# Key sums as three additions and a reordered opening, in an attention and spectral-gate kernel on Trainium2

## The chip, the core and the metric

The kernel runs on one core of one Trainium2 chip. A core has TensorE (PE in the profile; its weight loads are PEld), VectorE (DVE), ScalarE (ACT), GpSimd (POOL) and the queue engine SyncE (SP), which here issues most DMA transfers. The metric is the device time of one execution in microseconds (us); a run's time is compared by the median over runs.

## The reference, cut to what matters

```
q, k, v: (4, 8, 768, 64)                    # batch, heads, tokens, head size
k_rep = k.reshape(4, 8, 12, 64, 64).mean(axis=3)        # one mean key per block of 64 tokens
gate = einsum("bhsd,bhnd->bhsn", q, k_rep)               # causal over blocks
mask: each token sees its 3 best blocks by gate and its own block, causally
attn = softmax(q @ k^T / 8 where mask) @ v
x = attn as (4, 768, 512)
x1, x2, x3 = split(x @ w_proj)
y = x1 * irfft(rfft(x2) * rfft(filter)) * x3
out = y @ w_out
```

The mean keys need, for each head, the sum of the tokens of every block. How that sum is begun is one half of the change.

## The kernel before, in words

The four batches have eight heads each. Two heads make a *pair*; there are 16 pairs (0 to 15), and every pair is worked in six *slots* (two heads times three groups of score tiles), 96 slots in all. In a slot, `scores` makes score tiles on TensorE, `exponentials` (L441) takes them through ScalarE's exponential (L445) and GpSimd's causal cut (L448), and `products` (L454) multiplies them with the values on TensorE (L466). After the third group of a head, VectorE divides by the row sums into `xnat` (L474, L475), which frees the accumulator. When all four pairs of a batch are done, the steps of `hyena` for that batch are put between the slots of the next one: matrix products, transforms with cosine and sine matrices, and products on VectorE and GpSimd (L541 to L558, L574, L594).

The preparation of a pair runs some slots ahead of it, by three lists written out by hand (`early`, `bank`, `fills`) that the slot loop empties: `prep_k16` (L304), `prep_k` (L316), `prep_kr` (L339), `prep_q` (L347), `prep_gate` (L374), `prep_mask` (L387), `prep_turn` (L400) and `prep_v` (L335). The order of the instructions on every engine is the program's order.

Keys arrive in `k_nat` as 96 partitions by 2 heads by 8 tokens by 64 numbers (each partition has eight neighbouring tokens). `prep_k16` does two things with them: a cast to 16 bits in `k16` (L309 on GpSimd, for pair 0 L311 on ScalarE), and the sum over the eight tokens in `ks` (L313, one `tensor_reduce` on VectorE over a view in which the token is innermost, with a stride of 64 numbers). `prep_k` multiplies `ks` with block indicators on TensorE (L319, `krp`), turns `k16` by transposes (L326, `kt`), copies them with ScalarE to `KH` (L329), and puts two transfers into a list `late` that copy `KH` to the score operands KA (first head) and KB (second head). `flush` issues what the list holds, on SP's queue. The score operands have 64 rows of keys or queries and 12 more: on the keys' side block indicators (`erow`, L199 to L204), on the queries' side the mask. The queries' operands are TQ (first head) and QB (second head); for pairs 0 and 1 QB's rows are copied from PSUM directly (L361 to L370), for the others by a transfer (L372).

The opening is written out in L90 to L222 and L635 to L666. It loads the first keys, queries, second keys and first values, makes small tables on GpSimd (`blk`, `half1`, `biasr`, `ownm`, `erow`), and the sine matrix FS in three parts: `sine_products` on TensorE and a rounding step on VectorE (L137), `sine_multiple` on GpSimd (L144), and `sine_rest`, a product on TensorE (L149) and the sine on ScalarE (L150). `warm(n)` is n products of zeros on TensorE (L100). `constants_late` is ten small VectorE instructions (L209 to L220). `second_buffers` (L663) sends `erow` to KA[1], KB[1] and KB[2] in slot 0 on SP's queue.

The tile `hsb` of the filter's spectrum (L274) has the tag `h0` or `h1` in a pool of two buffers, in slots 16 to 25.

Of the kernel before, what the change touches and what calls it, by code (L numbers as in the profile page):

```python
# [18 lines left out]
def kernel(  # L19
# [10 lines left out]
    nc = tc.nc  # L30

    B, H, S, D = q.shape
    P = 128
    SC = S // P
    NB = S // 64
# [39 lines left out]
    def load(p, what):  # L75
        b, dc = divmod(p, DC)
        src = {"k": k, "q": q, "v": v}[what]
        if what == "k":

            t = nat.tile([SE, 2, 8, D], FP32, name="k_nat", tag="k_nat", bufs=2)  # L80
            for h in range(2):
                nc.sync.dma_start(t[:, h], src[b, 2 * dc + h].rearrange("(p e) d -> p e d", e=8))
            nats[what, p] = t
            return
        t = nat.tile([P, SC, 2, D], FP32, name=what + "_nat", tag=what + "_nat")
        for h in range(2):
            nc.sync.dma_start(t[:, :, h, :], src[b, 2 * dc + h].rearrange("(c p) d -> p c d", p=P))
        nats[what, p] = t

    for p, w in ((0, "k"), (0, "q"), (1, "k"), (0, "v")):  # L90
        load(p, w)


# [36 lines left out]
    def sine_products(i):  # L130
        if i != 1:
            sine["t"] = sc_tile()
        pr = sine["t"][:, 512 * (i % 2):512 * (i % 2) + F]
        nc.tensor.matmul(pr, lhsT=tvals[:, P * i:P * (i + 1)], rhs=fvals, start=True, stop=False,
                         skip_group_check=True)
        ka = hy.tile([P, F], FP32, name="dft_ka", tag=f"t{i % 2 + 1}", bufs=3)
        nc.vector.tensor_scalar(ka, in0=pr, scalar1=1.0 / S2, scalar2=MAGIC,  # L137
                                op0=ALU.mult, op1=ALU.add)
        sine[i] = pr, ka

    def sine_multiple(i):
        pr, ka = sine[i]
        kw = hy.tile([P, F], fp, name=f"dft_kw{i}", tag="gg", bufs=2 * DC)
        nc.gpsimd.tensor_scalar(kw, in0=ka, scalar1=-MAGIC, scalar2=1.0, op0=ALU.add, op1=ALU.mult)  # L144
        sine[i] = pr, kw

    def sine_rest(i):
        pr, kw = sine.pop(i)
        nc.tensor.matmul(pr, lhsT=idn, rhs=kw, start=False, stop=True, skip_group_check=True)  # L149
        nc.scalar.activation(FS[:, i, :], pr, AF.Sin, bias=0.0, scale=TWO_PI / S2)  # L150

    nc.scalar.activation(tw, twf, AF.Sin, bias=0.0, scale=math.pi / S)
    for i in range(HC):
        sine_products(i)
    warm(5)

    idn = const.tile([P, P], fp, name="idn")
    nc.gpsimd.tensor_scalar(idn, in0=id32, scalar1=-float(S2), scalar2=0.0, op0=ALU.mult, op1=ALU.add)
    par = const.tile([P, 1], FP32, name="par")
    nc.gpsimd.iota(par, pattern=[[1, 1]], base=0, channel_multiplier=1,  # L160
                   allow_small_or_imprecise_dtypes=True)
    for i in range(HC):
        sine_multiple(i)
    blk = const.tile([SE, NB], FP32, name="blk")
    nc.gpsimd.memset(blk, 1.0)
    nc.gpsimd.affine_select(out=blk, in_=blk, compare_op=ALU.is_ge, fill=0.0, base=0,
# [13 lines left out]
    nc.gpsimd.memset(half1[0:1, :], 1.0)  # L180
    nc.gpsimd.memset(half1[32:33, 64:128], 1.0)
    biasr = const.tile([P, SC - 1, 2, NB], BF16, name="biasr")
    nc.gpsimd.memset(biasr, 0.0)
    for c in range(1, SC):
        nc.gpsimd.memset(biasr[0:1, c - 1, :, 2 * c + 1:NB], -CBIG)
        nc.gpsimd.memset(biasr[32:33, c - 1, :, 2 * c + 1:2 * c + 2], CBIG)

    MN = [const.tile([P, SC, P], fp, name=f"MN{i}") for i in range(2)]
    V16 = [const.tile([P, SC, 2, 66], fp, name=f"V16_{i}") for i in range(3)]
# [2 lines left out]
    TQ = [const.tile([P, S], fp, name=f"TQ{i}") for i in range(2)]  # L192
    QB = [const.tile([P, S], fp, name=f"QB{i}") for i in range(2)]
    ownm = const.tile([P, SC - 1, 2, NB], fp, name="ownm")
    nc.gpsimd.memset(ownm, 1.0)
    for c in range(1, SC):
        for hf in range(2):
            nc.gpsimd.memset(ownm[64 * hf:64 * hf + 64, c - 1, :, 2 * c + hf:2 * c + hf + 1], 0.0)
    erow = KA[0][64:64 + NB, :]  # L199
    nc.gpsimd.memset(erow, MKEY)  # L200
    nc.gpsimd.affine_select(out=erow, in_=erow, compare_op=ALU.is_ge, fill=0.0, base=0,
                            pattern=[[1, S]], channel_multiplier=-64)
    nc.gpsimd.affine_select(out=erow, in_=erow, compare_op=ALU.is_ge, fill=0.0, base=63,
                            pattern=[[-1, S]], channel_multiplier=64)  # L204

    def constants_late():
        parh = const.tile([P, 1], FP32, name="parh")
# [11 lines left out]
        nc.vector.memset(tw0[0:1, 0:1], 0.0)  # L219
        nc.vector.memset(tw0[0:1, 1:2], 1.0 / S)  # L220

    nc.vector.memset(MN[0], 0.0)  # L222
    sgn = const.tile([P, 1], FP32, name="sgn")
    tw0 = const.tile([P, 2], FP32, name="tw0")
    flip = const.tile([P, P], FP32, name="flip")
# [68 lines left out]
    state = {}  # L294
# [9 lines left out]
    def prep_k16(p):  # L304
        kn = nats["k", p]
        k16 = hp.tile([SE, 8, 2, D], fp, name="k16", tag="k16")
        src = kn.rearrange("p h e d -> p e h d")
        if p:
            nc.gpsimd.tensor_copy(k16, src)  # L309
        else:  # L310
            nc.scalar.copy(k16, src)  # L311
        ks = small.tile([SE, 2, D], FP32, name="ks", tag="ks")
        nc.vector.tensor_reduce(out=ks, in_=kn.rearrange("p h e d -> p h d e"), axis=AX.X, op=ALU.add)  # L313
        state["k", p] = k16, ks

    def prep_k(p):  # L316
# [30 lines left out]
    def prep_q(p, t):  # L347
        qn = nats["q", p]
        tq = TQ[p % 2]
        if t == 0:  # L350
            state["ql", p] = hp.tile([P, S], fp, name="ql", tag="ql")
        ql = state["ql", p]
        qt = turned_pair("qt", qn, t)
        cols = slice(F * t, F * (t + 1))
        nc.scalar.activation(tq[:, cols], qt, AF.Copy, bias=0.0, scale=QS)  # L355
        lo = P if t == 0 else 0
        nc.vector.scalar_tensor_tensor(out=ql[:, F * t + lo:F * (t + 1)], in0=qt[:, lo:F],  # L357
                                       scalar=QS, in1=tq[:, F * t + lo:F * (t + 1)],
                                       op0=ALU.mult, op1=ALU.subtract)
        if p < 2:  # L360
            def direct():  # L361
                if p:
                    nc.vector.tensor_scalar(QB[p][0:D, cols], in0=qt[D:P, :], scalar1=QS,
                                            scalar2=None, op0=ALU.mult)
                else:
                    nc.scalar.activation(QB[p][0:D, cols], qt[D:P, :], AF.Copy, bias=0.0, scale=QS)
            if p:
                direct()
            else:
                state["direct", t] = direct  # L370
        elif t == 1:
            late.append(lambda: nc.sync.dma_start(QB[p % 2][0:D, :], tq[D:P, :]))  # L372

    def prep_gate(p):  # L374
# [25 lines left out]
    def prep_turn(p):  # L400
        mn, tq, qb = MN[p % 2], TQ[p % 2], QB[p % 2]
        mt = one("mt", (P, SC, P), fp)
        for c in range(SC):
            nc.tensor.transpose(mt[:, c, :], mn[:, c, :], id16)  # L404
        if p < 2:
            flat = mt.rearrange("p c s -> p (c s)")
            nc.scalar.activation(tq[64:64 + NB, :], flat[64:64 + NB], AF.Copy, bias=0.0, scale=MQ)
            nc.vector.tensor_scalar(qb[64:64 + NB, :], in0=flat[96:96 + NB], scalar1=MQ,
                                    scalar2=None, op0=ALU.mult)
        else:  # L410
            m16 = hp.tile([P, S], fp, name="m16", tag="m16")
            nc.scalar.activation(m16[64:108, :], mt[64:108].rearrange("p c s -> p (c s)"),  # L412
                                 AF.Copy, bias=0.0, scale=MQ)
            late.append(lambda: (nc.sync.dma_start(tq[64:64 + NB, :], m16[64:64 + NB, :]),
                                 nc.sync.dma_start(qb[64:64 + NB, :], m16[96:96 + NB, :])))
# [216 lines left out]
        for f in todo:  # L632
            f()

    sine_rest(0)  # L635
    prep_k16(0)
    prep_k(0)
    flush()
    load(1, "q")
    prep_kr(0)  # L640
    prep_q(0, 0)
    prep_q(0, 1)
    sine_rest(1)
    sine_rest(2)
    nc.scalar.preload_act_table_set("natural_log_exp_and_others")
    prep_gate(0)
    prep_mask(0)
    state.pop(("direct", 0))()
    state.pop(("direct", 1))()
    for p, w in ((2, "k"), (1, "v"), (2, "q")):  # L650
        load(p, w)
    warm(8)
    prep_turn(0)
    warm(4)
    constants_late()
    nc.gpsimd.tensor_copy(KB[0][64:64 + NB, :], erow)
    for t in V16:
        nc.gpsimd.memset(t[:, :, :, D:D + 2], 1.0)
    prep_v(0)
    prep_k16(1)  # L660
    scores(0)

    def second_buffers():  # L663
        for t in (KA[1], KB[1], KB[2]):
            nc.sync.dma_start(t[64:64 + NB, :], erow)
        nc.vector.memset(MN[1], 0.0)  # L666


    early = [[] for _ in range(slots + 1)]
# [36 lines left out]
                at(bank, n0 + 8, lambda p=p: turn_x(p))  # L706
            at(early, n0 + 10, lambda p=p: fold(p))

    early[0].append(second_buffers)
    early[1].append(make_flip)  # L710
    early[3].append(cosines)
    for i in range(HC):
# [99 lines left out]
```

## Time and profile before

| | |
|---|---|
| runs, us | 297.91, 297.96, 302.45 (median 297.96) |
| profiled execution, us | 295.79 |
| its span, first to last instruction, us | 294.1 |
| busy: TensorE, VectorE, ScalarE, GpSimd, us | 247.2, 196.4, 171.0, 153.5 |
| share of the chain that ended last: TensorE, VectorE | 46%, 31% |
| first score product, first exponential, us from the start | 15.95, 16.53 |
| mean granted clock of TensorE | 0.95 |

The page of the profile gives the engines' busy times, the span in 40 slices, the chain of work that ended last (followed back from the last instruction, at each step to what released it) and the costliest groups of instructions. A group's row has the line, engine, operation, tile written and tiles read, partitions by elements, the count, the busy time in all and the mean of one in ns, and then the idle time of the engine in front of them and what ended it. A row of a timeline has start and duration in us, engine, line, operation and tiles. A row of the chain in order of time has start, duration, engine and line.

### The profile page before, as it was taken

The page shows a single profiled execution, that of the slowest core. Times are in us where ns is not written, and L with a number is a line of the kernel's source. Part 1 is how long each engine was busy: PE and PEld are TensorE (multiplying, and loading weights), DVE is VectorE, ACT ScalarE, POOL GpSimd, SP SyncE. Part 2 cuts the span into 40 slices and gives each one's busy share as a digit, 9 for nine tenths or more (in the row PEclk, how much of TensorE's full clock was granted, in tenths as well). Part 3 has the DMA queues.
Part 4 walks back from the last instruction along what each step waited for, and adds up shares of the span by engine and source line. Part 5 has one row for each costly group of instructions (what it writes and reads, how often), then busy time and mean ns, then how long its engine had stood idle before and what let it go on. Part 6 is the DMA issues. An engine that isn't in the chain of part 4 may idle for free.

```text
span 294.1 us, 6382 instructions
## 1 busy us (share of the span) xinstructions
PE 247.2 (84%) x2300; PEld 153.3 (52%) x2300; DVE 196.4 (67%) x531; ACT 171.0 (58%) x260; POOL 153.5 (52%) x285
## 2 busy tenths in 40 slices
PE   7869878868597969898979789889899998988874
PEld 1547655545464536555555466656455664534431
DVE  5477877769745996867186959593759764237580
ACT  2736594757284627586846467768665675442323
POOL 6835352659471757765324667672326876004740
PEclk9985798989599999999999999999999999999998
DMA  7585967666687755377845344477631102400005
GB/s 185 113 167 153 240 178 155 133 133 144 133 148 160 135 114 141 75 147 205 231 97 139 69 123 113 112 182 229 136 83 45 34 8 66 171 0 0 2 0 214
DMA packets 71991, 36.11 MB, mean 123 GB/s; under 512 B 59684, under 2 KB 65048, under 8 KB 71960
## 3 DMA queue, kind: packets, MB, share of 16 engines
q1 hardware_dynamic: 69704, 33.62, 46.1%
q0 software_dynamic: 2256, 2.10, 5.3%
q8 instruction: 18, 0.29, 0.4%
q14 instruction: 13, 0.11, 0.1%
HBM read 24.64 MB, written 6.29 MB: 105 GB/s over the span
## 4 chain that ended last, share of the span: by engine, by line
PE 46%; DVE 31%; ACT 11%; issue 6%; DMA 2%; POOL 2%; SPq 1%; POOLq 0%; DVEq 0%; ACTq 0%
DVE ks L313 6%; PE sps L436 6%; PE op L601 5%; PE o L466 4%; PE x1p L586 4%; PE x3p L589 4%; PE x2p L524 4%; ACT ex L445 4%; DVE m L392 3%; DVE xnat L475 3%; PE kt L326 2%; DVE ql L357 2%; PE qt L300 2%; PE xx L536 2%; DVE yy L574 2%
## 5 line engine op out<-in xcount | busy, mean ns | idle before, releaser
L445 ACT ACTIVATE ex<-sps 128x896 f16<-128x896 f32 x96 | 87.4, 925 | 3.9 <-PE sps L436 3.9
L448 POOL TENSOR_SCALAR_AFFINE_SELECT ex<-ex 128x256 f16<-128x256 f16 x96 | 39.8, 416 | 88.4 <-ACT ex L445 65.0
L466 PEld LDWEIGHTS <-ex 128*128 128x128 f16 x672 | 33.8, 101 | 36.0 <-DVE xnat L475 21.6
L466 PE MATMUL o<-V,ex 128*128 128x65 f16 x672 | 38.7, 199 | 13.7 <-DVE xnat L475 12.7
L436 PE MATMUL sps<-QB,KB 76*128 76x512 f16 (+1 forms) x144 | 28.2, 307 | 4.1 <-ACT ex L445 4.1
L313 DVE TENSOR_REDUCE ks<-k_nat 96x128 f32<-96x1024 f32 x16 | 30.7, 1922 | 0.0
L547 POOL TENSOR_TENSOR PQ<-ta 128x512 f16<-128x512 f32 x12 | 15.2, 1268 | 26.8 <-DVE ta L546 26.8
L412 ACT ACTIVATE m<-mt 44x768 f16<-44x768 f16 x14 | 11.3, 806 | 30.1 <-PE mt L404 30.0
L436 PE MATMUL sps<-TQ,KA 76*128 76x512 f16 (+1 forms) x144 | 27.2, 300 | 1.9 <-DMA TQ<-m 1.1
L601 PE MATMUL op<-wo,yT 128*128 128x512 f16 x96 | 24.2, 379 | 3.4 <-POOL yT L556 3.4
L524 PE MATMUL x2p<-wp,xf 128*128 128x512 f16 x96 | 24.3, 379 | 0.8 <-DVE xf L503 0.8
L357 DVE SCALAR_TENSOR_TENSOR ql<-qt,TQ 128x256 f16<-128x256 f32 (+1 forms) x32 | 15.5, 485 | 13.1 <-ACT TQ L355 12.9
L355 ACT ACTIVATE TQ<-qt 128x384 f16<-128x384 f32 x32 | 15.7, 492 | 13.7 <-PE qt L300 13.4
L594 DVE TENSOR_TENSOR gg<-x1sb,x3p 128x384 f32<-128x384 f16 x24 | 13.2, 549 | 14.6 <-ACT x1sb L592 7.6
L556 POOL TENSOR_TENSOR yT<-gg,yy 128x384 f16<-128x384 f32 x16 | 16.0, 998 | 11.5 <-DVE yy L574 11.4
L586 PE MATMUL x1p<-xT,wp 128*128 128x384 f16 x96 | 19.5, 325 | 2.6 <-DVE tb L542 2.6
L592 ACT CAST x1sb<-x1p 128x384 f16<-128x384 f32 x24 | 11.5, 480 | 17.0 <-PE x1p L586 16.7
L604 ACT COPY osb<-op 128x512 f32<-128x512 f32 x24 | 14.1, 588 | 11.3 <-PE op L601 9.5
L589 PE MATMUL x3p<-xT,wp 128*128 128x384 f16 x96 | 19.5, 326 | 1.1 <-ACT x1sb L592 1.1
L436 PEld LDWEIGHTS <-KB 76*128 76x128 f16 x144 | 13.4, 102 | 12.0 <-issue 6.5
L329 ACT COPY KH<-kt 128x768 f16<-128x768 f16 x16 | 12.8, 799 | 10.5 <-PE kt L326 10.0
L475 DVE TENSOR_TENSOR xnat<-o,rc 128x384 f16<-128x384 f32 x32 | 17.9, 558 | 1.1
(162 smaller groups left out, 529.6 us busy)
## 6 DMA issues: line engine op xcount, KB each, us to landing
k_nat<-in_k_dram SPq DMA_DIRECT2D x32, 192.0 KB, 3.3
q_nat<-in_q_dram SPq DMA_DIRECT2D x32, 192.0 KB, 4.0
v_nat<-in_v_dram SPq DMA_DIRECT2D x32, 192.0 KB, 4.7
out_dram<-osb SPq DMA_DIRECT2D x24, 256.0 KB, 2.2
KA<-KH SPq DMA_DIRECT2D x16, 96.0 KB, 2.1
KB<-KH SPq DMA_DIRECT2D x16, 96.0 KB, 2.2
wp<-in_moe_w_proj_dram POOLq DMA_DIRECT2D x12, 128.0 KB, 3.9
QB<-TQ SPq DMA_DIRECT2D x14, 96.0 KB, 2.1
```

What stands on the lines that cost most here:

```text
L313: nc.vector.tensor_reduce(out=ks, in_=kn.rearrange("p h e d -> p h d e"), axis=AX.X, op=ALU.add)
L357: nc.vector.scalar_tensor_tensor(out=ql[:, F * t + lo:F * (t + 1)], in0=qt[:, lo:F], scalar=QS, in1=tq[:, F * t + lo:F * (t + 1)], op0=ALU ...
L436: nc.tensor.matmul(t[:, col:col + q1 - q0], lhsT=kk[0:64 + NB, P * kc:P * (kc + 1)], rhs=qq[0:64 + NB, q0:q1], start=True, stop=True, skip ...
L445: nc.scalar.activation(ex, t[:, 0:W], AF.Exp, bias=0.0, scale=EXPS)
L448: nc.gpsimd.affine_select(out=tri, in_=tri, compare_op=ALU.is_ge, fill=0.0, base=0, pattern=[[0, 2], [1, P]], channel_multiplier=-1)
L466: nc.tensor.matmul(o[:, qc, :], lhsT=ex[:, c0:c0 + P], rhs=V16[p % 3][:, kc, h, 0:65], start=first, stop=False, skip_group_check=True)
L475: nc.vector.tensor_tensor(xn[:, :, D * h:D * (h + 1)], o[:, :, 0:D], rc.to_broadcast([P, SC, D]), op=ALU.mult)
L524: nc.tensor.matmul(pa, lhsT=xf[:, eo, dc, P * i:P * (i + 1)], rhs=wp[:, dc, Dm:2 * Dm], start=(dc == 0), stop=(dc == DC - 1))
L556: nc.gpsimd.tensor_mul(st["yT"][:, dc, 0:F], g, yy[:, 0, :])
L586: nc.tensor.matmul(x1p, lhsT=wp[:, d2, dsl], rhs=xT[:, d2, hs], start=(d2 == 0), stop=(d2 == DC - 1))
L589: nc.tensor.matmul(x3p, lhsT=wp[:, d2, 2 * Dm + P * dc:2 * Dm + P * (dc + 1)], rhs=xT[:, d2, hs], start=(d2 == 0), stop=(d2 == DC - 1))
L601: nc.tensor.matmul(op, lhsT=st["yT"][:, cc, P * i:P * (i + 1)], rhs=wo[:, cc, :], start=(cc == 0), stop=(cc == DC - 1))
```

## The change

It has two halves.

The sum over eight tokens becomes three additions of halves: tokens 0 to 3 and 4 to 7 into a tile `k4` (512 numbers a partition, from the pool and tag of `hsb`'s first buffer), its halves into `k2` (256), and those into `ks` (128). The cast of pair 0's keys goes from ScalarE to GpSimd, like that of the other pairs.

The opening is written in another order. Loads: first queries, first keys, second keys, first values, second queries. The rounding step of the sines goes from VectorE to ScalarE. The tables `biasr` and `ownm` go from GpSimd to VectorE, with the zeros of MN[0] behind them. The sines' multiples come behind the first keys' cast, and the queries' transposes ahead of the keys' product. The three `sine_rest` come behind the first gates and masks. `erow`, its copy to KB[0] and `par` come behind these (`mask_rows`). QB's rows of pairs 0 and 1 go by a transfer like the others'. The mask rows of TQ for pair 0 are copied by VectorE. There are fewer warm-up products (3, 4 and 2 in place of 5, 8 and 4). The three transfers of `erow` to the other operands are issued in slots 1, 4 and 7.

```diff
-    for p, w in ((0, "k"), (0, "q"), (1, "k"), (0, "v")):
+    for p, w in ((0, "q"), (0, "k"), (1, "k"), (0, "v"), (1, "q")):
         load(p, w)
...
-        nc.vector.tensor_scalar(ka, in0=pr, scalar1=1.0 / S2, scalar2=MAGIC,
-                                op0=ALU.mult, op1=ALU.add)
+        nc.scalar.activation(ka, pr, AF.Copy, bias=MAGIC, scale=1.0 / S2)
...
-    warm(5)
+    warm(3)
...
-    for i in range(HC):
-        sine_multiple(i)
...
-    nc.gpsimd.memset(biasr, 0.0)
+    nc.vector.memset(biasr, 0.0)
     for c in range(1, SC):
-        nc.gpsimd.memset(biasr[0:1, c - 1, :, 2 * c + 1:NB], -CBIG)
-        nc.gpsimd.memset(biasr[32:33, c - 1, :, 2 * c + 1:2 * c + 2], CBIG)
+        nc.vector.memset(biasr[0:1, c - 1, :, 2 * c + 1:NB], -CBIG)
+        nc.vector.memset(biasr[32:33, c - 1, :, 2 * c + 1:2 * c + 2], CBIG)
...
-    nc.gpsimd.memset(ownm, 1.0)
+    nc.vector.memset(ownm, 1.0)
...
+    nc.vector.memset(MN[0], 0.0)
...
+    def mask_rows():
+        nc.gpsimd.memset(erow, MKEY)
+        nc.gpsimd.affine_select(out=erow, in_=erow, compare_op=ALU.is_ge, fill=0.0, base=0,
+                                pattern=[[1, S]], channel_multiplier=-64)
+        nc.gpsimd.affine_select(out=erow, in_=erow, compare_op=ALU.is_ge, fill=0.0, base=63,
+                                pattern=[[-1, S]], channel_multiplier=64)
+        nc.gpsimd.tensor_copy(KB[0][64:64 + NB, :], erow)
+        nc.gpsimd.iota(par, pattern=[[1, 1]], base=0, channel_multiplier=1,
+                       allow_small_or_imprecise_dtypes=True)
...
-        if p:
-            nc.gpsimd.tensor_copy(k16, src)
-        else:
-            nc.scalar.copy(k16, src)
+        nc.gpsimd.tensor_copy(k16, src)
         ks = small.tile([SE, 2, D], FP32, name="ks", tag="ks")
-        nc.vector.tensor_reduce(out=ks, in_=kn.rearrange("p h e d -> p h d e"), axis=AX.X, op=ALU.add)
+        k4 = hy2.tile([SE, 2, 4, D], FP32, name="k4", tag="h0")
+        k2 = small.tile([SE, 2, 2, D], FP32, name="k2", tag="k2", bufs=1)
+        nc.vector.tensor_add(k4, kn[:, :, 0:4], kn[:, :, 4:8])
+        nc.vector.tensor_add(k2, k4[:, :, 0:2], k4[:, :, 2:4])
+        nc.vector.tensor_add(ks, k2[:, :, 0], k2[:, :, 1])
...
-        if p < 2:
-            def direct():
-                if p:
-                    nc.vector.tensor_scalar(QB[p][0:D, cols], in0=qt[D:P, :], scalar1=QS,
-                                            scalar2=None, op0=ALU.mult)
-                else:
-                    nc.scalar.activation(QB[p][0:D, cols], qt[D:P, :], AF.Copy, bias=0.0, scale=QS)
-            if p:
-                direct()
-            else:
-                state["direct", t] = direct
-        elif t == 1:
+        if t == 1:
             late.append(lambda: nc.sync.dma_start(QB[p % 2][0:D, :], tq[D:P, :]))
...
-            nc.scalar.activation(tq[64:64 + NB, :], flat[64:64 + NB], AF.Copy, bias=0.0, scale=MQ)
+            if p:
+                nc.scalar.activation(tq[64:64 + NB, :], flat[64:64 + NB], AF.Copy, bias=0.0, scale=MQ)
+            else:
+                nc.vector.tensor_scalar(tq[64:64 + NB, :], in0=flat[64:64 + NB], scalar1=MQ,
+                                        scalar2=None, op0=ALU.mult)
...
-    sine_rest(0)
     prep_k16(0)
+    for i in range(HC):
+        sine_multiple(i)
+    prep_q(0, 0)
+    prep_q(0, 1)
     prep_k(0)
     flush()
-    load(1, "q")
     prep_kr(0)
-    prep_q(0, 0)
-    prep_q(0, 1)
-    sine_rest(1)
-    sine_rest(2)
-    nc.scalar.preload_act_table_set("natural_log_exp_and_others")
     prep_gate(0)
     prep_mask(0)
-    state.pop(("direct", 0))()
-    state.pop(("direct", 1))()
+    for i in range(HC):
+        sine_rest(i)
+    nc.scalar.preload_act_table_set("natural_log_exp_and_others")
+    mask_rows()
     for p, w in ((2, "k"), (1, "v"), (2, "q")):
         load(p, w)
-    warm(8)
+    warm(4)
     prep_turn(0)
-    warm(4)
+    warm(2)
     constants_late()
-    nc.gpsimd.tensor_copy(KB[0][64:64 + NB, :], erow)
...
-    early[0].append(second_buffers)
+    early[0].append(lambda: nc.vector.memset(MN[1], 0.0))
+    for i, t in enumerate((KA[1], KB[1], KB[2])):
+        early[3 * i + 1].append(lambda t=t: buffer_rows(t))
```

More of the change, by code (lines that the diff above doesn't have):

```diff
@@ L154 @@
         sine_products(i)
-    warm(5)
+    warm(3)
     idn = const.tile([P, P], fp, name="idn")
     nc.gpsimd.tensor_scalar(idn, in0=id32, scalar1=-float(S2), scalar2=0.0, op0=ALU.mult, op1=ALU.add)
-    par = const.tile([P, 1], FP32, name="par")
-    nc.gpsimd.iota(par, pattern=[[1, 1]], base=0, channel_multiplier=1,
-                   allow_small_or_imprecise_dtypes=True)
-    for i in range(HC):
-        sine_multiple(i)
     blk = const.tile([SE, NB], FP32, name="blk")
@@ L194 @@
     ownm = const.tile([P, SC - 1, 2, NB], fp, name="ownm")
-    nc.gpsimd.memset(ownm, 1.0)
+    nc.vector.memset(ownm, 1.0)
     for c in range(1, SC):
         for hf in range(2):
-            nc.gpsimd.memset(ownm[64 * hf:64 * hf + 64, c - 1, :, 2 * c + hf:2 * c + hf + 1], 0.0)
+            nc.vector.memset(ownm[64 * hf:64 * hf + 64, c - 1, :, 2 * c + hf:2 * c + hf + 1], 0.0)
+    nc.vector.memset(MN[0], 0.0)
     erow = KA[0][64:64 + NB, :]
[L200 to L204, printed above, removed]
+    par = const.tile([P, 1], FP32, name="par")
+    def mask_rows():
[7 more added lines that the diff above has]
+                       allow_small_or_imprecise_dtypes=True)
     def constants_late():
@@ L220, in constants_late @@
         nc.vector.memset(tw0[0:1, 1:2], 1.0 / S)
-    nc.vector.memset(MN[0], 0.0)
     sgn = const.tile([P, 1], FP32, name="sgn")
@@ L661, with buffer_rows @@
     scores(0)
[L663 to L666, printed above, removed]
+    def buffer_rows(t):
+        nc.sync.dma_start(t[64:64 + NB, :], erow)
     early = [[] for _ in range(slots + 1)]
```

## The prediction, made before the result

> **What bounds the kernel now.** I read the page's parts 1, 2, 4 and 5, then the chain in order of time, then the timelines of VectorE (DVE) and GpSimd (POOL) around the lines that the diff touches. First the page:
>
> ```profile
> span 294.1 us, 6382 instructions
> ...
> PE 247.2 (84%) x2300; PEld 153.3 (52%) x2300; DVE 196.4 (67%) x531; ACT 171.0 (58%) x260; POOL 153.5 (52%) x285
> ...
> PE 46%; DVE 31%; ACT 11%; issue 6%; DMA 2%; POOL 2%; SPq 1%; POOLq 0%; DVEq 0%; ACTq 0%
> DVE ks L313 6%; PE sps L436 6%; PE op L601 5%; PE o L466 4%; PE x1p L586 4%; PE x3p L589 4%; PE x2p L524 4%; ACT ex L445 4%; DVE m L392 3%; DVE xnat L475 3%; PE kt L326 2%; DVE ql L357 2%; PE qt L300 2%; PE xx L536 2%; DVE yy L574 2%
> ...
> L313 DVE TENSOR_REDUCE ks<-k_nat 96x128 f32<-96x1024 f32 x16 | 30.7, 1922 | 0.0
> ```
>
> TensorE is the busiest engine, but the chain that ended last is handed between it and VectorE. Its largest single line is L313, the reduction that the change replaces: 16 of 1.92 us. In the chain in order of time it stands whole nine times (pairs 1, 3, 5, 6, 7, 8, 11, 12, 15) and in part twice more (9 and 13). How it bounds, at pair 7:
>
> ```profile
> 86.22 1.95 DVE ks L313
> 88.17 0.79 DVE m L392 x10
> ...
> 90.27 0.57 DVE xnat L475
> ...
> 90.88 0.39 PE o L466 x7
> ```
>
> The reduction stands on VectorE ahead of the gate maxima and of `xnat`, and TensorE waits for `xnat` to free its accumulator. What the reduction gains or loses there, the span gains or loses.
>
> **The three additions, alone.** They process 512, 256 and 128 elements per partition instead of 1024. No row has exactly such an addition; the nearest are VectorE's two-tensor operations in float32:
>
> ```profile
> L594 DVE TENSOR_TENSOR gg<-x1sb,x3p 128x384 f32<-128x384 f16 x24 | 13.2, 549 | 14.6 <-ACT x1sb L592 7.6 <-PE x3p L589 7.0
> L541 DVE TENSOR_TENSOR ta<-xx,Asb 128x512 f32<-128x512 f32 x9 | 6.2, 686 | 1.1 <-PE xx L536 1.1
> ```
>
> From 384 to 512 elements is 137 ns, 1.07 ns an element, with about 140 ns fixed. So the additions take 0.69, 0.41 and 0.28 us; each needs the one before, and such a step costs 0.04 us (0.15 us operations follow each other by 0.19 in the rows of L209 below). Sum 1.46 us, a gain of about 0.45 us on each reduction. Eleven on the chain would give 5 us.
>
> The Trainium skill ("VectorE: DVE Perf Modes", Rules for kernel authors) calls `tensor_reduce` the slowest VectorE operation and advises restructuring it; by that alone the change is the 5 us gain, and rival A below is that case.
>
> **The three additions, beside GpSimd.** This decides. An addition reads two tensors in SBUF; the reduction read one. Look at what the trace has of VectorE operations with two SBUF inputs:
>
>
> ```profile
> 278.92 1.06 DVE L558 TENSOR_TENSOR yT<-gg,yy 128x384 f16<-128x384 f32 x1
> ...
> 285.54 0.56 DVE L558 TENSOR_TENSOR yT<-gg,yy 128x384 f16<-128x384 f32 x1
> ```
>
> ```profile
> 278.57 1.00 POOL L556 TENSOR_TENSOR yT<-gg,yy 128x384 f16<-128x384 f32 x1 [1.88 <-DVE yy L574]
> ```
>
> ```profile
> 66.66 0.93 DVE L289 SCALAR_TENSOR_TENSOR A<-hsb,tw,turn 128x512 f16<-128x512 f32 x1
> ```
>
> ```profile
> 66.64 0.41 POOL L448 TENSOR_SCALAR_AFFINE_SELECT ex<-ex 128x256 f16<-128x256 f16 x1 [0.46 <-DMA QB<-m]
> 66.99 1.28 POOL L337 CAST V<-v_nat 128x768 f16<-128x768 f32 x1
> ```
>
> The same L558 takes 0.56 us alone and 1.06 where GpSimd works: it ends at 279.98, 0.41 us after GpSimd's 279.57, and 0.4 us is the streaming of its 384 elements. L289 ends 0.54 us after GpSimd's 67.05, the streaming of 512. Then GpSimd's cast, begun at 66.99, takes 1.28 us and ends 0.68 after VectorE. So the two engines do not share: the one that comes second waits for the other's whole instruction, then streams. The reductions, beside the same GpSimd work, all take 1.77 to 1.96 us:
>
> ```profile
> L319 PE MATMUL krp<-blk,ks x32: 232/259/386, 7.6 to 214.6; 96*128 96x12 f32 x32
> L313 DVE TENSOR_REDUCE ks<-k_nat x16: 1769/1938/1956, 5.7 to 208.4; 96x128 f32<-96x1024 f32 x16
> ```
>
> (per line: shortest, median and longest in ns, first and last start in us).
>
> The Trainium skill ("SBUF — State Buffer", Who interferes with whom) states just this: a VectorE instruction with two SBUF inputs and a GpSimd instruction that reads SBUF take an exclusive lock, and a reduction never does. The trace agrees by the rows above.
>
> Now the changed line's own place. `prep_k16` puts GpSimd's cast of the same keys (L309) beside the sum, so the two meet by construction. Pairs 7, 8 and 9:
>
> ```profile
> 86.61 0.40 POOL L448 TENSOR_SCALAR_AFFINE_SELECT ex<-ex 128x256 f16<-128x256 f16 x1 [1.31 <-ACT ex L445]
> 86.96 1.03 POOL L309 CAST k<-k_nat 96x1024 f16<-96x1024 f32 x1
> ```
>
> ```profile
> 101.61 1.95 DVE L313 TENSOR_REDUCE ks<-k_nat 96x128 f32<-96x1024 f32 x1
> ```
>
> ```profile
> 101.14 1.27 POOL L549 TENSOR_TENSOR PQ<-tb 128x512 f16<-128x512 f32 x1
> ```
>
> ```profile
> 118.11 1.96 DVE L313 TENSOR_REDUCE ks<-k_nat 96x128 f32<-96x1024 f32 x1
> ```
>
> ```profile
> 117.34 1.00 POOL L556 TENSOR_TENSOR yT<-gg,yy 128x384 f16<-128x384 f32 x1
> 118.30 1.01 POOL L558 TENSOR_TENSOR yT<-gg,yy 128x384 f16<-128x384 f32 x1
> ```
>
> I let the earlier comer go first. After a wait GpSimd has about 0.13 us of its instruction behind it (the cast above: 0.68 left of the usual 0.82), so L448 takes 0.27 more, L309 0.90 and L558 0.87; VectorE's additions take 0.54, 0.28 and 0.14 after a wait. Times from the start of the sum:
> - Pair 7: first addition to 0.69, L448 to 0.96, second to 1.24; the third is issued at 1.28, but L309 has been waiting and goes to 2.14; third to 2.28. Against 1.94: 0.34 lost. Pairs 5, 6, 11 and 15 have the same neighbours: 5 x 0.34 = 1.7 us.
> - Pair 8: L549 holds until 0.81; first to 1.35, L448 1.62, second 1.90, L309 2.80, third 2.94: 1.0 lost. Pair 12 is alike: 2.0 us.
> - Pair 9: L556 until 0.23; first 0.77, L558 1.64, second 1.92, L448 2.19, third 2.33: 0.39 lost; pair 13 alike: 0.8 us.
> - Pair 3 has two casts of 0.2 us ahead of L309 that let the third addition through: a gain of 0.35.
>
> Sum over the pairs behind the opening: +4.1 us. GpSimd ends its cast some 0.4 us later, hidden: the keys are transposed two slots later. Bounds: no meeting at all gives -0.45 x 10 = -4.5; GpSimd first at every meeting gives +8.4 (rival B). I take +4.1, by the rows' own order.
>
> **The opening.** These rows carry it:
>
> ```profile
> 0.81 0.87 SPq L82 DMA_DIRECT2D k_nat<-in_k_dram  x2
> ...
> 1.73 1.02 SPq L87 DMA_DIRECT2D q_nat<-in_q_dram  x2
> ...
> 13.67 0.82 DVE L398 TENSOR_TENSOR MN<-lt,ownm 128x120 f16<-128x120 f16 x1
> ...
> 15.93 0.56 DVE L408 TENSOR_SCALAR QB<-mt 12x768 f16<-12x768 f16 x1 [1.44 <-ACT TQ L407]
> 15.95 0.92 PE L436 MATMUL sps<-TQ,KA 76*128 76x512 f16 x6
> ...
> 16.50 0.15 DVE L209 TENSOR_SCALAR parh<-par 128x1 f32<-128x1 f32 x1
> ...
> 16.69 0.15 DVE L210 TENSOR_SCALAR parh<-parh 128x1 f32<-128x1 f32 x1
> ...
> 17.78 1.87 DVE L313 TENSOR_REDUCE ks<-k_nat 96x128 f32<-96x1024 f32 x1
> ...
> 19.70 0.60 PE L319 MATMUL krp<-blk,ks 96*128 96x12 f32 x2 [2.83 <-DVE ks L313]
> ```
>
> ```profile
> k_nat<-in_k_dram SPq DMA_DIRECT2D x32, 192.0 KB, 3.3
> q_nat<-in_q_dram SPq DMA_DIRECT2D x32, 192.0 KB, 4.0
> ```
>
> - Loads on SP's queue: queries go first, so the first keys' second half is issued at about 0.81 + 1.02 + 0.45 = 2.3 and lands 3.3 to 4.0 later, near 6.0. The second queries join the first batch (two issues, 1.02 us of the queue that waits for nothing). The key sum starts at 6.0 instead of 5.7, beside the keys' cast, which moves from ScalarE to GpSimd and collides: first addition 6.7, cast 7.6, second 7.9, a sine multiple between, third 8.4. The key product krp follows near 8.4 instead of 7.6: 0.8 late.
> - The gates make this up, because the queries' transposes and TQ copies are done before the keys come, and two sine products, two sines and the two QB copies of ScalarE leave the way. I estimate them 1 us earlier than before. The mask product MN took 0.82 us for 120 elements: it waited for the GpSimd copy of `erow` that ran then (L656). `mask_rows` keeps that copy and four more instructions on GpSimd behind the sine multiples, so this wait can stay.
> - Ahead of the mask's transpose now stand three sine products and 4 warm-up matmuls; before, 8 warm-ups stood there. The mask rows of TQ go by VectorE (0.56 by L408) instead of by ScalarE, and VectorE then writes QB's. First scores near 14.9, 1 us earlier; bounds 1 us later (keys or the KA transfer late) and 3 us earlier.
> - The tables on VectorE: 22 memsets and MN's, some 2.2 us, fill its idle time before 6.0. Cover gone, they would push the key sum by as much.
> - The sum of pair 1 has GpSimd's cast behind it already and gains its 0.45, and meets one L448 of 0.4: net about +0.3 gained. With the scores' 1 us, the next key product comes at 18.4 instead of 19.70.
> - Pair 1's QB copies (two on VectorE) become a transfer, needed nine slots on and hidden:
>
> ```profile
> 23.79 0.56 DVE QB L363
> ...
> 24.97 0.56 DVE QB L363
> ```
>
> Both are on the chain, 1.1 us; but TensorE runs at half clock there and is busy almost throughout (next fence), so I count 0.6. The three row transfers on SP in slots 1, 4 and 7 instead of at once are due later than that and count nothing.
>
> ```profile
> 19.15:32.80 13.65, 12.58 (x108) 10.04 (x109) 10.03 (x28) 7.94 (x11) 5.02 (x14) 0.50 0.54 140
> ```
>
> Opening: -1.3 (19.70 to 18.4) - 0.6 = -1.9, with bounds of +1 and -4.5. **Sum:** +4.1 - 1.9 = +2.2 us on the profiled execution (295.79 us, span 294.1). That lies 2.2 us below the median of the runs, 297.96, which is what the forecast is made against: 300 us.
>
> **Rivals.**
> A, faster: the meetings cost nothing, because the additions come before or behind GpSimd's work, or the third slips in ahead of the cast. For it: the reduction is the chain's largest line, and the opening shortens. Against: the cast is issued by the same function, and began within 1.5 us of the sum in the rows above. Time: 297.96 - 4.5 - 1.9 = 291.5, the point at which it passes 2% being that nearly all ten sums gain.
> B, slower: at each boundary GpSimd's next instruction goes before the waiting addition. Pair 7's second addition then waits for L309 too and ends its sum at 2.46 (0.5 lost), pair 8's at 3.3 (1.3), pair 9's first waits for L558 as well: 3.6 (1.7). 5 x 0.5 + 2 x 1.3 + 2 x 1.7 = 8.5 us; with the opening's -1.9, 304.5, past 2% when more than four fifths of the meetings go so. For it: L558 begins 0.04 us before L556 ends (118.30 against 118.34). Against: L289 above got in between two GpSimd instructions.
> C, no net change by another way: the clock. TensorE stood still from 16.87 to 19.70 ahead of the half-clock stretch above. If the shorter wait keeps the clock up, its 12.58 busy us shrink and perhaps 3 us go: 297. If the longer sums open such gaps later, they come back. The Trainium skill ("TensorE: Matmul & The Clock Gate", What's actually happening) says that about one idle window of 3.4 us halves the clock; here 2.83 us were enough or nearly so.
>
> **How the numbers follow.** Forecast (meetings in the rows' order, 296 to 303): 0.45. A: 0.2, 291.5. B: 0.2, 304.5. C: 0.15, 297. A time within 2% of 297.96 (292 to 303.9) is about what cannot be told from no change. Faster by over 2%: A's 0.2. Slower: 0.22, B and a little of the forecast's upper end. Same: 0.58. The range runs from 291.5 to 304.5, from A's place to B's.
>
> **What would show it.** Right: the second and third additions' mean well above 0.41 and 0.28 us, with the third ending just behind L309; the three together about 2.3 us in pairs 7 and 11, near 2.9 in pairs 8 and 12; GpSimd's L309 or L448 longer than 1.03 and 0.41; first scores near 15 us. Wrong: additions at 0.69, 0.41, 0.28 throughout and no additions on the chain (A); the first addition over 1.2 us in pair 9 (B); another clock in the first 33 us (C).

## The result, and the profile after

The changed kernel takes 306.86 us in the median of 4 runs (305.24 to 309.93), the kernel before 297.94 (297.41 to 302.45). The ratio is 1.029, with a 95% interval of 1.020 to 1.037: slower. Here and below a median is over all runs of a kernel, and a ratio compares undisturbed executions alone, which is why the two need not agree (in e5 they are 2% apart). The changed kernel was run once more as experiment e0: 305.89 us, ratio 1.030 (1.023 to 1.037). The first profiled execution took 309.93 us, the longest of its four, with a span of 308.2 us and a mean granted clock of 0.911; that of e0 has a span of 304.2 us at 0.943, and the profile before 294.1 us at 0.950.

The page after, first profile:

```profile
span 308.2 us, 6396 instructions
...
PE 256.7 (83%) x2292; PEld 160.0 (52%) x2292; DVE 202.1 (66%) x581; ACT 169.8 (55%) x259; POOL 160.1 (52%) x264
...
PE 46%; DVE 30%; ACT 8%; issue 5%; DMA 3%; POOL 1%; POOLq 0%; SPq 0%; DVEq 0%; ACTq 0%
...
L308 POOL CAST k<-k_nat 96x1024 f16<-96x1024 f32 x16 | 18.5, 1157 | 1.5 <-DMA k_nat<-in_k_dram 1.5
```

VectorE's busy time rose by 5.7 us, although its largest line was to become shorter. The three additions, in VectorE's groups with the shapes kept apart:

```profile
L312 DVE TENSOR_TENSOR k<-k_nat 96x512 f32<-96x512 f32 x16 | 12.7, 791 | 2.2 <-DMA k_nat<-in_k_dram 1.8 <-issue 0.4
L314 DVE TENSOR_TENSOR ks<-k 96x128 f32<-96x128 f32 x16 | 12.1, 756 | 0.6
L313 DVE TENSOR_TENSOR k<-k 96x256 f32<-96x256 f32 x16 | 12.0, 753 | 0.5
```

They have 512, 256 and 128 elements and cost nearly the same, 0.79, 0.75 and 0.76 us. That is the mark of a wait inside an instruction: 16 sums take 36.8 us of VectorE in all, the 16 reductions took 30.7. The smallest addition shows why. VectorE's and GpSimd's timelines at pair 7 (start, duration, engine, line):

```profile
94.03 0.68 DVE L312 TENSOR_TENSOR k<-k_nat 96x512 f32<-96x512 f32 x1
94.74 0.51 DVE L313 TENSOR_TENSOR k<-k 96x256 f32<-96x256 f32 x1
95.28 1.01 DVE L314 TENSOR_TENSOR ks<-k 96x128 f32<-96x128 f32 x1
```

```profile
94.42 0.56 POOL L442 TENSOR_SCALAR_AFFINE_SELECT ex<-ex 128x256 f16<-128x256 f16 x1 [2.52 <-ACT ex L439]
94.93 1.22 POOL L308 CAST k<-k_nat 96x1024 f16<-96x1024 f32 x1
```

The third addition, 0.28 us of work, lasts 1.01 us and ends at 96.29, 0.14 us after the cast. The cast itself lasts 1.22 instead of 1.03 us and ends 0.90 us after the second addition (95.25), as one that waited for it would. The sum takes 2.26 us; 2.28 was forecast. The tile `k4`, which shares a buffer with `hsb`, is no cause: from pair 3 on VectorE is never idle ahead of the first addition.

The loss takes the path by which the reduction bounded the kernel: TensorE's waits for `xnat` grew from 12.7 to 18.5 us, in the profile before and in e0's (who waits, for whom: us in all, times, longest):

```profile
PE o L466 <- DVE xnat L475: 12.7, 13, 3.7
```

```profile
PE o L460 <- DVE xnat L469: 18.5, 14, 5.2
```

Where did the time come from? The table takes the start of the exponential (L445 before, L439 after) in a slot as a time mark in both kernels, for e0's profile against the profile before. A stretch's figure is how much longer it took.

| stretch | longer by, us | what is in it |
|---|---|---|
| start to slot 0 | +0.53 | the opening |
| slot 0 to 24 | +0.64 | pairs 1 to 5 summed, QB copies gone |
| slot 24 to 30 | +3.88 | sum of pair 6: 4.40 us against 1.92; granted clock 0.66 against 0.79 |
| slot 30 to 33 | +0.31 | sum of pair 7: 2.26 |
| slot 36 to 39 | +2.45 | sum of pair 8: 2.94 |
| slots 54 to 57, 66 to 69 and 78 to 81 | +0.33, +0.38, +0.32 | sums of pairs 11, 13 and 15 |
| slot 42 to 45 | +0.36 | sum of pair 9: 2.32 |
| slot 60 to 63 | +0.99 | sum of pair 12: 2.94 |
| the rest | -0.12 | |

They add up to the 10.07 us between the spans. Nearly all of it lies where a sum stands, and nothing of it behind the sum of pair 15. In two stretches the sum isn't all of it.

In slots 24 to 30 the sum grew by 2.48 us. The other 1.40 us go with the lower clock: the same 133 matmuls kept TensorE busy for 13.62 us instead of 11.50. The row of e0, then that of before (length, busy time of TensorE, its weight loads, VectorE, ScalarE, GpSimd; granted clock; DMA):

```profile
72.00:91.91 19.91, 13.62 (x133) 9.48 (x129) 12.04 (x30) 9.11 (x14) 10.91 (x21) 0.66 0.67 123
```

```profile
70.83:86.87 16.04, 11.50 (x133) 8.54 (x133) 10.61 (x29) 9.07 (x15) 10.37 (x21) 0.79 0.73 137
```

Pairs 8 and 12 do the same work and have the same sums, yet one stretch is 1.46 us longer. TensorE's granted clock is the difference. The stretches of slots 36 to 39 and 60 to 63 of e0:

```profile
107.15:120.28 13.13, 9.64 (x88) 5.86 (x86) 10.03 (x27) 5.02 (x8) 6.45 (x9) 0.87 0.52 112
171.40:183.07 11.67, 8.15 (x88) 5.06 (x86) 9.94 (x27) 5.02 (x8) 6.46 (x9) 1.00 0.41 96
```

And the same slots before:

```profile
101.79:112.47 10.68, 8.05 (x88) 5.00 (x86) 9.01 (x25) 5.02 (x8) 5.76 (x9) 1.00 0.67 139
162.90:173.58 10.68, 8.05 (x88) 5.00 (x86) 9.01 (x25) 5.02 (x9) 5.76 (x9) 1.00 0.44 105
```

In both pairs VectorE works 1 us longer, which is the additions' wait (2.94 against 1.95 us). Only at pair 8 was the longer standstill of TensorE followed by a stretch at lower clock, and its matmuls then took 1.5 us more.

Pair 6 is the worst place, in the first profile too:

```profile
76.38 1.58 DVE L313 TENSOR_TENSOR k<-k 96x256 f32<-96x256 f32 x1
77.99 1.79 DVE L314 TENSOR_TENSOR ks<-k 96x128 f32<-96x128 f32 x1
```

```profile
75.93 0.67 POOL L442 TENSOR_SCALAR_AFFINE_SELECT ex<-ex 128x256 f16<-128x256 f16 x1
76.56 1.03 POOL L308 CAST k<-k_nat 96x1024 f16<-96x1024 f32 x1
77.54 0.55 POOL L242 DMA_DIRECT2D wp<-in_moe_w_proj_dram  x1
78.10 0.42 POOL L442 TENSOR_SCALAR_AFFINE_SELECT ex<-ex 128x256 f16<-128x256 f16 x1
78.49 0.69 POOL L286 TENSOR_SCALAR turn<-hsb,tw 128x512 f32<-128x512 f32 x1
79.14 0.58 POOL L242 DMA_DIRECT2D wp<-in_moe_w_proj_dram  x1
```

GpSimd's instructions come without a pause here. The third addition, 0.28 us of work, lasts 1.79 and ends at 79.78, 0.06 us after the last of the four GpSimd instructions that ended while it stood: each time the next of them went ahead of it. Two of the four are issues of transfers.

### The profile page after: what moved, and what is told of

It is laid out like the page before. It is cut to its first block, busy times and chain, and to the rows that moved or that the text cites. A ratio compares the mean times of both kernels' runs of the same rounds, so it can differ in the third digit from the quotient of the medians.

```text
span 308.2 us, 6396 instructions
## 1 busy us (share of the span) xinstructions
PE 256.7 (83%) x2292; PEld 160.0 (52%) x2292; DVE 202.1 (66%) x581; ACT 169.8 (55%) x259; POOL 160.1 (52%) x264
## 4 chain that ended last, share of the span: by engine, by line
PE 46%; DVE 30%; ACT 8%; issue 5%; DMA 3%; POOL 1%; POOLq 0%; SPq 0%; DVEq 0%; ACTq 0%
PE sps L430 7%; PE op L595 5%; PE o L460 5%; PE x2p L518 4%; PE x3p L583 4%; PE x1p L580 4%; DVE ks L314 3%; DVE k L312 3%; ACT ex L439 3%; DVE m L382 3%; DVE k L313 2%; DVE xnat L469 2%; PE kt L327 2%; PE xx L530 2%; DVE yy L568 2%
## 5 line engine op out<-in xcount | busy, mean ns | idle before, releaser
L442 POOL TENSOR_SCALAR_AFFINE_SELECT ex<-ex 128x256 f16<-128x256 f16 x96 | 43.6, 456 | 96.8 <-ACT ex L439 74.8
L439 ACT ACTIVATE ex<-sps 128x896 f16<-128x896 f32 x96 | 87.4, 926 | 3.2 <-PE sps L430 3.1
L460 PEld LDWEIGHTS <-ex 128*128 128x128 f16 x672 | 35.3, 104 | 41.6 <-DVE xnat L469 25.5
L460 PE MATMUL o<-V,ex 128*128 128x65 f16 x672 | 40.3, 203 | 18.7 <-DVE xnat L469 17.9
L430 PE MATMUL sps<-QB,KB 76*128 76x512 f16 (+1 forms) x144 | 30.7, 328 | 3.1 <-ACT ex L439 3.1
L430 PE MATMUL sps<-TQ,KA 76*128 76x512 f16 (+1 forms) x144 | 28.4, 310 | 0.7 <-DMA TQ<-m 0.4
L518 PE MATMUL x2p<-wp,xf 128*128 128x512 f16 x96 | 25.1, 389 | 0.8 <-DVE xf L497 0.8
L358 DVE SCALAR_TENSOR_TENSOR ql<-qt,TQ 128x256 f16<-128x256 f32 (+1 forms) x32 | 15.4, 484 | 13.3 <-ACT TQ L356 13.1
L583 PE MATMUL x3p<-xT,wp 128*128 128x384 f16 x96 | 20.3, 336 | 1.1 <-ACT x1sb L586 1.1
L430 PEld LDWEIGHTS <-KB 76*128 76x128 f16 x144 | 14.3, 109 | 12.0 <-issue 7.0
L308 POOL CAST k<-k_nat 96x1024 f16<-96x1024 f32 x16 | 18.5, 1157 | 1.5 <-DMA k_nat<-in_k_dram 1.5
L300 PE MATMUL qt<-id,q_nat 128*128 128x128 f32 x96 | 19.0, 319 | 0.0
```

Of the source, the lines that this page charges most:

```text
L300: nc.tensor.transpose(y[:, P * c:P * (c + 1)], x[:, HC * t + c].rearrange("p h d -> p (h d)"), id32)
L430: nc.tensor.matmul(t[:, col:col + q1 - q0], lhsT=kk[0:64 + NB, P * kc:P * (kc + 1)], rhs=qq[0:64 + NB, q0:q1], start=True, stop=True, skip ...
L439: nc.scalar.activation(ex, t[:, 0:W], AF.Exp, bias=0.0, scale=EXPS)
L442: nc.gpsimd.affine_select(out=tri, in_=tri, compare_op=ALU.is_ge, fill=0.0, base=0, pattern=[[0, 2], [1, P]], channel_multiplier=-1)
L460: nc.tensor.matmul(o[:, qc, :], lhsT=ex[:, c0:c0 + P], rhs=V16[p % 3][:, kc, h, 0:65], start=first, stop=False, skip_group_check=True)
L518: nc.tensor.matmul(pa, lhsT=xf[:, eo, dc, P * i:P * (i + 1)], rhs=wp[:, dc, Dm:2 * Dm], start=(dc == 0), stop=(dc == DC - 1))
```

## The experiments

Theory L: the additions read two tensors in SBUF and wait for GpSimd's instructions, and these waits, with the lower clock that follows some of them, are the loss. Rival O: the reordered opening is the loss. Rival C, called theory C below: TensorE's clock alone.

**e0, the changed kernel again.**

> The changed kernel once more, for a second profile. Theory L (the additions wait for GpSimd's instructions and these waits are the loss): 305 to 308 us, with sums of 2.26 us at pairs 7, 11, 15, about 2.9 at 8 and 12 and 2.3 at 9 and 13, as in the first profile. Theory C (TensorE's clock is the loss; it stood at half for 54.6 us in the first profile, 27.3 us before): where the half-clock stretches are shorter here, the time falls towards 298.

305.89 us (ratio 1.030). The sums are as in the first profile: 2.26 us at pairs 7, 11 and 15, 2.94 at 8 and 12, 2.32 at 9 and 13. The mean clock was 0.943, against 0.950 in the profile before, and the span was still 10 us longer. The clock alone is not the cause; it adds to it, as the stretches of pairs 6 and 8 show.

**e1, the additions alone,** in the kernel before:

```diff
-        nc.vector.tensor_reduce(out=ks, in_=kn.rearrange("p h e d -> p h d e"), axis=AX.X, op=ALU.add)
...
+        nc.vector.tensor_add(k4, kn[:, :, 0:4], kn[:, :, 4:8])
+        nc.vector.tensor_add(k2, k4[:, :, 0:2], k4[:, :, 2:4])
+        nc.vector.tensor_add(ks, k2[:, :, 0], k2[:, :, 1])
```

> The kernel before with the three additions alone; opening as before. Theory L: it carries the loss: 304 to 306 us (sums on the chain: 6.4 us longer by the first profile, about 1 more where a longer wait halves the clock). Rival O (the reordered opening is the loss): 297 to 299.

306.98 us, ratio 1.033 (1.024 to 1.042), as much as the changed kernel lost. The whole loss is here.

**e2, the opening alone:** the changed kernel with the reduction put back (the diff of e1 reversed).

> The changed kernel with the reduction put back; the opening as changed. Theory L: 297 to 299 us, since slot 0's exponential came at 16.57 against 16.53. Rival O: 304 to 307.

297.85 us, ratio 1.005 (1.000 to 1.010). Rival O falls. The opening gains nothing either; it was to gain 1.9.

**e3, the cast away from the additions:**

```diff
-        nc.gpsimd.tensor_copy(k16, src)
+        def cast():
+            nc.gpsimd.tensor_copy(k16, src)
+        if p < 3:
+            cast()
+        else:
+            at(early, 2 * NS * p - 12, cast)
```

> The changed kernel with GpSimd's cast of the keys one slot later than the additions, from pair 3 on; all else as changed. Theory L: the third addition meets no cast: sums near 1.55 us at pairs 5, 6, 7, 11, 15, near 2.1 at 8 and 12, still 2.3 at 9 and 13; 0.4 x 5 gained against the reduction, 0.2 x 2 + 0.4 x 2 lost: 296 to 299 us. Theory C or O: no more than 2 us below the changed kernel, 304 to 307.

300.52 us, ratio 1.011 (1.006 to 1.017): more than 5 us of the loss are gone with the cast of each pair moved, though it is still above the kernel before, and 1.5 us over the range given. The additions by group, and at pair 7:

```profile
L317 DVE TENSOR_TENSOR k<-k_nat 96x512 f32<-96x512 f32 x16 | 12.9, 804 | 2.7 <-DMA k_nat<-in_k_dram 2.3 <-issue 0.4
L318 DVE TENSOR_TENSOR k<-k 96x256 f32<-96x256 f32 x16 | 11.0, 686 | 0.5
L319 DVE TENSOR_TENSOR ks<-k 96x128 f32<-96x128 f32 x16 | 5.4, 337 | 0.6
```

```profile
88.54 0.68 DVE L317 TENSOR_TENSOR k<-k_nat 96x512 f32<-96x512 f32 x1
89.25 0.51 DVE L318 TENSOR_TENSOR k<-k 96x256 f32<-96x256 f32 x1
89.80 0.29 DVE L319 TENSOR_TENSOR ks<-k 96x128 f32<-96x128 f32 x1
```

The third addition fell from 0.76 to 0.34 us in the mean, the first stayed: it meets other GpSimd work. The sums are 1.54 us at pairs 5, 7, 11 and 15, and 2.3 at 9 and 13, as theory L had it (1.55 and 2.3). At 8 and 12 they are 2.31 instead of 2.1, and pair 6 came to 1.91 instead of 1.55. Of the time left over the kernel before, the stretch of pair 8 has 1.76 us and that of pair 12 0.36, with the same sums: again the lower clock (0.86 and 1.00). Slots 18 to 30 have another 3.4 us, at a lower clock than before; e2, with the reduction, has 2.7 there, so most of that doesn't come from the additions.

**e4, the reduction behind `xnat`.** From pair 3 on, in the kernel before, `prep_k16` is split: the cast stays, the sum goes to the last list of the next slot (argument 1 is the cast alone, 0 the sum alone). Its reader, the keys' product, is one slot behind it now, where it was two. The calls that change, without the split itself:

```diff
...
-                at(early, k_at - 2, lambda p=p: prep_k16(p))
+                at(early, k_at - 2, lambda p=p: prep_k16(p, 1))
+                at(bank, k_at - 1, lambda p=p: prep_k16(p, 0))
...
```

> The kernel before with the reduction taken out of its place ahead of the gate maxima and xnat, and put behind xnat in the next slot's last list (pairs 3 to 15); the cast stays. It tests the step that the place in the chain gives the sum its weight: if so, with the same 1.94 us it becomes cheaper, TensorE's waits for xnat (12.7 us in all before) shrink by 4 to 8 us, 290 to 294 us. If VectorE's total work is what counts: 297 to 299.

299.81 us, ratio 1.000 (0.996 to 1.005). No gain, but a different profile. TensorE's waits for the sum before, and then those of e4:

```profile
PE krp L319 <- DVE ks L313: 3.2, 2, 2.8
```

```profile
PE krp L323 <- DVE ks L317: 13.5, 9, 2.8
PE o L470 <- DVE xnat L479: 5.9, 11, 1.5
```

The waits for `xnat` fell from 12.7 to 5.9 us, and the key product in the following slot now waits 13.5 us for the sum, where it waited 3.2. The execution profiled took 302.71 us at a mean clock of 0.926, the longest of e4's, so the sizes of its waits may be above those of a run at the median.

**e5, the same with the additions.**

> The same with the three additions in place of the reduction, so that the cast comes a slot before them. Theory L: what is left are meetings with the causal cuts and products on GpSimd; sums between 1.5 and 2.3 us, mean near the reduction's 1.94, so within 1 us of the run with the reduction behind xnat. If the additions only suffer from the cast: 2 to 4 us below it.

304.82 us in the median, ratio 1.004 (0.999 to 1.008). The sums are 1.45 us at seven of the thirteen pairs from 3 on, 2.3 to 2.9 at the other six (5, 6, 8, 9, 12, 13), 29.5 us in all against the reductions' 30.2. Its executions run from 298.11 us at a clock of 0.942 to 305.67 us at 0.908. The ratio is that of e4 within its interval; the median lies 5 us above e4's, where 1 us was expected. How the two compare is not decided more closely than by the two intervals.

**e6, no warm-up ahead of the mask's transpose.** The changed opening with the reduction, less one `warm(4)`.

> The changed opening with the reduction, without the 4 warm-up products ahead of the first mask's transpose. The mask was ready at 13.04 us in the changed kernel (14.49 before) but its transposes came at 14.32 behind these products (1.92 us at half clock). If they ate the opening's gain, the first exponential comes near 15.3 instead of 16.6 and the time falls by about 1 us, to 296.5 to 297.5, unless TensorE's clock is granted later for it: then 298 to 301.

297.54 us, ratio 1.001 (0.997 to 1.005). The first exponential came at 14.71 us, 1.8 earlier than before, and in the profile the lead was gone by slot 18. The same stretch of e6, then of e2, with the granted clock third from the end:

```profile
10.74:38.05 27.31, 23.97 (x203) 17.92 (x204) 19.14 (x67) 15.31 (x22) 11.04 (x26) 0.50 0.69 176
```

```profile
10.74:38.05 27.31, 20.31 (x221) 14.09 (x221) 19.95 (x73) 16.37 (x23) 11.30 (x27) 0.94 0.75 176
```

In the same 27 us TensorE of e6 ran at half clock throughout and did 203 matmuls, that of e2 221. (The clock entries of e2's trace begin at 16.3 us, and an earlier stretch counts as 1.00.) So the warm-ups did delay the first scores, and in this execution the clock took the lead away. But it is the longest of e6's ten, 300.66 us at a mean clock of 0.906. The other nine took 297.24 to 298.71 us, and five of them ran at 0.96 or more: that leaves at most some 24 us at half clock in the whole run, less than the 27 us of the profile's opening. These five took 297.24 to 297.50 us, where e2's profile with its 0.965 took 297.35. So a half clock as in the profile can't be what took the lead in them, and what did is not shown.

**e7, the keys' product one slot later too,** on top of e4:

```diff
-            at(bank, k_at, lambda p=p: prep_k(p))
+            at(bank, k_at + (1 if p > 2 else 0), lambda p=p: prep_k(p))
```

> As e4 (reduction behind xnat), and the product and transposes of the keys (prep_k) one slot later too, from pair 3 on. In e4 TensorE's waits for xnat had turned into waits for the key sum ahead of krp, 0.8 to 2.7 us at each of eleven pairs. If these were what ate its gain, they go and 4 to 10 us with them: 288 to 294 us. If another wait comes in their place, 296 to 300.

284.52 us, ratio 0.954 (0.949 to 0.959): faster than both kernels, and 3.5 us below the range given. The page and TensorE's waits:

```profile
span 281.1 us, 6384 instructions
...
PE 243.6 (87%) x2300; PEld 149.8 (53%) x2300; DVE 195.1 (69%) x531; ACT 171.0 (61%) x260; POOL 155.4 (55%) x285
```

```profile
PE o L470 <- DVE xnat L479: 5.8, 12, 1.5
PE sps L440 <- ACT ex L449: 3.9, 7, 0.8
PE krp L323 <- DVE ks L317: 3.5, 3, 2.8
```

VectorE does the same work as before (195.1 us against 196.4) with the same reductions (30.5 us). The waits for `xnat` stay short and those for `ks` are back at 3.5 us; behind slot 27 the profile has no stretch at half clock before the last microseconds. Of the 12.9 us between the two spans 7.2 lie behind slot 30, spread over nearly every stretch there, and 4.3 in slots 24 to 30, where the kernel before has a granted clock of 0.79 and e7 one of 1.00.

**e8, e7 with the three additions.**

> The same with the three additions. Theory L: sums of 1.45 us where GpSimd leaves VectorE alone and 2.3 or more where it doesn't (pairs 5, 6, 8, 9, 12, 13 in e5), in the mean close to the reduction: within 2 us of e7. Were the additions simply a shorter sum: 2 to 5 us below it.

285.13 us, ratio 0.956 (0.953 to 0.959), within e7's interval. The sums cost 29.5 us against 30.5.

**e9, the changed opening with e7's order.**

> The changed opening with the reduction, and e7's order (reduction behind xnat, keys' product one slot later). The opening alone was worth nothing (297.85 against 297.95), so 283 to 286 us, as e7; if a smoother start keeps TensorE's clock up, 281 to 283.

283.73 us, ratio 0.950 (0.945 to 0.956), the lowest median. It can't be told from e7.

**e10, the keys' product one slot later, alone.**

> The kernel before with only the keys' product one slot later; the reduction stays ahead of the gate maxima and xnat. The control to e4 and e7: krp did not wait there, so 296 to 299 us. If this alone gives e7's gain, then the place of the sum is not what mattered.

295.36 us, ratio 0.988 (0.984 to 0.992): a gain of 1%, a little more than expected, and about a quarter of e7's. Neither half of e7 alone has its gain. Stretch by stretch e10 has e7's gains where no sum stands (0.73 us in slots 33 to 36, 0.91 in 39 to 42, 0.94 in 45 to 54), and gives most of them back where one does (0.26 to 0.94 us longer than before); TensorE's waits for `xnat` are 15.4 us there. With the sum behind `xnat` these stretches got shorter too, by 0.08 to 0.31 us.

## Why the prediction was wrong

The mechanism, additions that wait for GpSimd, was right; the sum built on it, +4.1 - 1.9 = +2.2 us, was too small in three terms: the meeting of pair 6, the opening, and the clock. Point by point:

- *The additions alone, 0.69, 0.41 and 0.28 us:* right. Where GpSimd left VectorE alone they took 0.69, 0.42 and 0.29 (pair 1), and 1.45 to 1.48 in all.
- *The wait for GpSimd, by the order of the rows:* right in kind and nearly everywhere in size. Forecast and measured sums: pair 7 2.28 and 2.26 us, pair 8 2.94 and 2.94, pair 9 2.33 and 2.32, pair 3 a gain of 0.35 and of 0.38. Rival A, that the meetings cost nothing, fell in e1. The rule of the Trainium skill ("SBUF — State Buffer", Who interferes with whom), that a two-input VectorE instruction and a GpSimd instruction that reads SBUF exclude each other for the whole instruction, holds in the rows of pair 7: 1.01 us for the third addition beside the cast, 0.29 in e3 without it.
- *Pair 6 "has the same neighbours" as pair 7:* wrong. It lost 2.3 us in the first profile and 2.5 in e0, where 0.34 was forecast. Behind its cast stand transfer issues and a product of the spectrum without a pause, and at each boundary GpSimd went ahead of the waiting addition. That is rival B's mechanism, at one pair; I had priced it for all or none. With it the meetings from pair 3 on that were counted cost 6.1 us in e0 (9 pairs lost 6.5, pair 3 gained 0.4), where the sum had +4.1.
- *The opening, -1.9 us:* wrong; e2 shows -0.1 (297.85 against 297.95). The mask product did come earlier (ready at 13.04 us in the first profile, instead of 14.49), but its transposes, at 14.32, stood behind four warm-up products, which I named and did not price. These took 1.92 us, as long as the eight before had (1.94), for each took 0.43 us instead of 0.22. First scores came at 15.90 us; 14.9 was forecast. e6 took these products away and had its first exponential 1.8 us earlier, but no less time in all; why is open. The range's upper end, rival B's 304.5, has these 1.9 us taken off as well: without them it is 306.4.
- *The clock, taken at nothing:* wrong, and with the opening the step by which the range failed. The additions' waits lengthen TensorE's standstills, and some of these were followed by 3.4 us or more at half clock. The lower clock goes with 1.46 us at pair 8 of e0 and with 1.40 us in the stretch of pair 6; the latter needn't come from the additions, since e2, with the reduction, is 1.47 us longer there too. The first two errors alone bring the forecast of +2.2 to about +6, or 304 us, which is still in the range; the rest up to the medians' 8 to 9 is of the size of one or two such stretches, which differ from run to run. That the standstills bring the low clock is argued from what followed them, and no run changed it alone. Rival C named gaps that longer sums could open, but only as what would cancel a gain; the sum has no term for them.
- *"What the reduction gains or loses there, the span gains or loses":* right for the loss. At pairs 7, 9, 11, 12, 13 and 15 the stretch grew by 0.31 to 0.99 us, within 0.02 us of the sum's growth. For a gain it holds only in part: in e3 the sums of pairs 7, 11 and 15 are 0.4 us shorter than the reduction and their stretches only 0.16.

What stays open: what decides, at a boundary between two GpSimd instructions, whether the waiting addition or the next instruction goes first. At pair 7 the addition went ahead of a transfer's issue that had begun before the cast ended, at pair 6 it did not.

## What to carry to other kernels

Before replacing a one-input operation by two-input ones on VectorE, look at what GpSimd does in the same microseconds: here a sum that is 0.45 us shorter alone became 0.3 to 2.5 us longer than the reduction at most pairs, since its own function issues a GpSimd cast beside it. The place in the order was worth more than the operation: the old reduction, put behind the work that TensorE waits for, with its reader moved one slot later as well, gave 4.6%. It took both moves, because the first alone only turned one wait into another. When two profiles differ, compare the granted clock stretch by stretch beside the waits, and look whether the profiled execution is one of the longer ones.

## What the runs showed of the hardware that I had not expected

A waiting VectorE instruction can be passed over more than once: at pair 6 an addition of 128 elements stayed 1.79 us behind four GpSimd instructions, two of them transfer issues of 0.55 and 0.58 us. And a standstill of TensorE can be followed by a stretch at half clock. e0's waits of TensorE ahead of the first product with the projection's weights (`x1p`) have two of 2.2 us, at pairs 8 and 12; then the two stretches of 3.4 us behind them (granted clock third from the end):

```profile
PE x1p L580 <- DVE tb L536: 4.4, 2, 2.2
```

```profile
112.77:116.18 3.41, 3.41 (x19) 1.77 (x18) 2.35 (x6) 0.53 (x1) 2.85 (x3) 0.50 0.18 35
176.90:180.30 3.40, 2.66 (x26) 1.59 (x25) 3.37 (x8) 1.46 (x2) 2.85 (x3) 1.00 0.14 27
```

The same standstill was followed by half clock once and by full clock once. In the first profile and in e1, which have the same two standstills of 2.21 us, both were followed by half clock (from 115.1 and 180.0 us, and from 111.3 and 176.2). The Trainium skill ("TensorE: Matmul & The Clock Gate", What's actually happening) has the clock fall after an idle window of about 3.4 us; here 2.2 us were followed by it in five places of six, and the wait of 1.3 us in the same place before was not followed by half clock at either pair (1.00 in the stretches of slots 36 to 39 and 60 to 63 above).
